# Decode attention over a 4096-long cache: the value blocks 1 to 30 are issued from ScalarE's DMA queue, the key blocks and the rest stay on SyncE's

## The chip, the cores and the metric

The kernel runs on one core of a Trainium2 chip. The metric is the device time of one execution in microseconds (us), median over several runs. Trace times below are microseconds from the start of the profiled execution's span. In the profile's rows PE is TensorE, PEld its weight loads, DVE is VectorE, ACT is ScalarE, POOL is GpSimd, and SP is SyncE, which here only issues DMAs. A row with a q behind the engine (SPq, ACTq) is the engine's instruction stream issuing a DMA, not the transfer itself.

## What is computed

One decode step of a transformer block: an adaptive layer norm, attention of 4 queries (one for each batch entry) with 32 heads of 128 over a cache of 4096 keys and values, an output projection, a second adaptive layer norm and a small SiLU feed-forward. All of it is float32.

```python
mod = (silu(c) @ w_mod).reshape(B, 6, 1, -1)        # B = 4
sa, ca, ga, sb, cb, gb = (mod[:, i] for i in range(6))
h = layernorm(x) * (1 + ca) + sa
q = (h @ wq).reshape(B, 1, H, Dh).transpose(0, 2, 1, 3)          # H = 32, Dh = 128
scores = einsum("bhqd,bhkd->bhqk", q, k_cache) * Dh ** -0.5      # 4096 keys
o = einsum("bhqk,bhkd->bhqd", softmax(scores), v_cache)
x = x + ga * (o.transpose(0, 2, 1, 3).reshape(B, 1, H * Dh) @ wo)
h = layernorm(x) * (1 + cb) + sb
x = x + gb * (silu(h @ w1) @ w2)
```

The caches are 268 MB each, and every byte of them is used once.

## The kernel before

The attention is cut into N = 32 blocks. Block n holds four heads (`t = n // 4`) of one batch entry (`b = n % 4`). Its keys `k{n}` and its values `v{n}` are each one load of 8 MiB: 128 partitions of 64 KB, where a partition holds 128 consecutive positions of one head. The function `load` issues such a load through `fetch` (L84).

**Slots.** All large data share one pool of three buffers of 64 KB a partition (tag `kv`, class `Slot`), handed out in turn. In order of time the slots go to `wm`, `wq`, `k0`, `v0`, `k1`, `v1`, `k2`, `v2` and so on, then `wo` and `w12`. So `v{n+1}` takes the slot of `k{n}`, and `k{n+2}` the slot of `v{n}`. A load is issued when the last reader of the slot's earlier content is done. That gives two moments in each block, named here R(n) and P(n):

- R(n): VectorE's last reduce of `k{n}` ends. Then `v{n+1}` can be issued.
- P(n): TensorE's last matmul on `v{n}` (`vsum`, L324) ends. Then `k{n+2}` can be issued.

**A block, step by step.** The key product is split by positions: VectorE multiplies positions 40 to 127 with the query (L271, the moment at which it starts is named S(n)) and reduces them (L276). GpSimd multiplies positions 0 to 39 (L271), and VectorE reduces these as well. At R(n) all scores are there. `rowmax`, `bmax` and `negmax` form the negative maximum, and `softexp` (L298) the exponentials on ScalarE, which GpSimd spreads into the zero-padded tiles `pz` (L302). TensorE multiplies 96 of the 128 value positions (`pv`, L339). For the first 32 positions GpSimd multiplies values by weights (L314) and adds them down in three steps (L318); `vsum` (L324) is TensorE's short end of it. After each second block `gather` (L350, L356) collects the output.

**Order.** The schedule is manual: every engine executes its instructions in the order in which the code emits them, and a waiting instruction holds up everything behind it on its engine. All loads of the caches and the weights are issued by SyncE. ScalarE issues four small loads of `c` at the start (L123), four small loads of `x` in block 28 (L404), and two of the four stores of the output. The loads of `wo` follow `v31`, and those of `w1` and `w2` come last.

Of the kernel before, what the change touches and what calls it, by code (L numbers as in the profile page):

```python
# [17 lines left out]
def kernel(  # L18
# [13 lines left out]
    nc = tc.nc  # L32
# [9 lines left out]
    NJ = HP * S // P  # L42
# [13 lines left out]
    N = B * NT  # L56
# [22 lines left out]
            names = " ".join(f"a{i}" for i in range(len(shape)))  # L79
            return v.rearrange(f"p ({names}) -> p {names}", **{f"a{i}": s for i, s in enumerate(shape)})  # L80

    def fetch(t, src, *cuts):
        for lo, hi in zip(cuts, cuts[1:]):
            nc.sync.dma_start(t[:, lo:hi], src[:, lo:hi])  # L84

    kt, vt = {}, {}

    def load(dst, cache, name, n, *cuts):
        t, b = divmod(n, B)
        dst[n] = Slot(f"{name}{n}").take(NJ, Dh)  # L90
        src = cache[b, HP * t : HP * (t + 1)].rearrange("h (p j) d -> (h p) j d", p=QW)
        fetch(dst[n], src, *(cuts or (0, NJ)))

    def load_k(n, *cuts):
        load(kt, kc, "k", n, *cuts)

    def load_v(n):
        load(vt, vc, "v", n)

    wmv = wm.rearrange("(p k) n -> p k n", p=P)  # L100
    wqv = wq.rearrange("(p k) n -> p k n", p=P)
# [26 lines left out]
    wqt = s1.take(NK, H * Dh)  # L128
    nc.sync.dma_start(wqt, wqv)
    load_k(0)  # L130

    ident = const.tile([P, P], F32, name="ident")
# [123 lines left out]
    def make_qb(n):  # L256
        if n % B == 0:
            m = work.tile([P, B, Dh], F32, tag="o", name=f"qm{n}", bufs=1)
            for b in range(B):
                nc.scalar.activation(m[:, b, :], qn, AF.Copy, scale=sel[:, n + b : n + b + 1])  # L260
            p = psum([P, B, Dh], "q", 2)
            nc.tensor.matmul(p, blk.rearrange("p i x -> p (i x)"), m, start=True, stop=True)
            for b in range(B):
                qb[n + b] = p[:, b, :]
        qw[n] = work.tile([P, Dh], F32, tag="qw", name=f"qw{n}")
        nc.scalar.activation(qw[n], qb[n], AF.Copy)  # L266
# [3 lines left out]
    def mult(eng, src, n, lo, hi):  # L270
        eng.tensor_mul(  # L271
            kt[n][:, lo:hi, :], kt[n][:, lo:hi, :], src[n].unsqueeze(1).to_broadcast([P, hi - lo, Dh])
        )

    def red(n, lo, hi):
        nc.vector.tensor_reduce(sc[n][:, lo:hi], kt[n][:, lo:hi, :], axis=AX.X, op=ALU.add)  # L276

    def rowmax(n):
        nm[n] = work.tile([P, 1], F32, tag="rm", name=f"rm{n}")
        nc.vector.tensor_reduce(nm[n], sc[n], axis=AX.X, op=ALU.max)  # L280

    def bmax(n):
        p = psum([P, P], "mx", 2)
        nc.tensor.transpose(p, nm[n].to_broadcast([P, P]), ident)  # L284
        nm[n] = p

    def negmax(n):
        m = work.tile([P, HP], F32, tag="hx", name=f"hx{n}")
        nc.vector.tensor_reduce(m, nm[n].rearrange("p (i x) -> p i x", i=HP), axis=AX.X, op=ALU.max)  # L289
        nc.vector.tensor_mul(m, m, hn)  # L290
        nm[n] = work.tile([P, 1], F32, tag="nm", name=f"nm{n}")
        nc.vector.tensor_reduce(nm[n], m, axis=AX.X, op=ALU.add)  # L292

    def softexp(n):
        t, b = divmod(n, B)
        if b == 0:
            rs[t] = work.tile([P, B], F32, tag="rs", name=f"rs{t}")
        nc.scalar.activation(sc[n], sc[n], AF.Exp, bias=nm[n], accum_out=rs[t][:, b : b + 1])  # L298
        for h in range(2):
            f = first(n) if h == 0 else 0  # L300
            m = HG - f
            nc.gpsimd.tensor_mul(  # L302
                pz[h][:, f * W : HG * W].rearrange("p (g x) -> p g x", g=m)[:, :, E:].rearrange("p g (i j) -> p g i j", i=HP),
                sc[n][:, JJ * (HG * h + f) : HG * JJ * (h + 1)].rearrange("p (g j) -> p g j", j=JJ)
                .unsqueeze(2).to_broadcast([P, m, HP, JJ]),
                hm.unsqueeze(1).unsqueeze(3).to_broadcast([P, m, HP, JJ]),
            )

    def first(n):
        return NV // JJ if n < N - 2 else 0  # L310

    def vmult(n):
        if first(n):
            nc.gpsimd.tensor_mul(  # L314
                vt[n][:, :NV, :], vt[n][:, :NV, :], sc[n][:, :NV].unsqueeze(2).to_broadcast([P, NV, Dh])
            )
            for m in (NV // 2, NV // 4, JJ):
                nc.gpsimd.tensor_add(vt[n][:, :m, :], vt[n][:, :m, :], vt[n][:, m : 2 * m, :])  # L318

    def vsum(n):  # L320
        t, b = divmod(n, B)
        q, a = divmod(b, 2)
        o = (1 - a) * E
        nc.tensor.matmul(  # L324
            po[t, q][0:W, :], hs[:, o : o + W], vt[n][:, :JJ, :].rearrange("p j d -> p (j d)"),
            start=False, stop=a == 1,
        )
# [20 lines left out]
    def gather(t, q):  # L348
        o = work.tile([P, JJ, Dh], F32, tag="o", name="o", bufs=1)
        nc.vector.tensor_mul(  # L350
            o, po[t, q].rearrange("p (j d) -> p j d", j=JJ), jm.unsqueeze(2).to_broadcast([P, JJ, Dh])
        )
        if q == 0:
            od[t] = psum([P, Dh], "od", 1)
        s = work.tile([P, Dh], F32, tag="lnu", name="s", bufs=1)
        nc.vector.tensor_reduce(s, o.rearrange("p j d -> p d j"), axis=AX.X, op=ALU.add)  # L356
        nc.tensor.matmul(od[t], spick[:, 2 - 2 * q : 2 - 2 * q + P], s, start=q == 0, stop=q == 1)  # L357
# [3 lines left out]
    def norm(t):  # L361
        p = psum([P, B], "mx", 2)
        nc.tensor.matmul(p, blk.rearrange("p i x -> p (i x)"), rs[t], start=True, stop=True)
        m = work.tile([P, B], F32, tag="dx", name="dx")
        nc.vector.tensor_mul(m, p, xm)
        rd[t] = work.tile([P, 2], F32, tag="rd", name="rd")
        nc.vector.tensor_reduce(rd[t][:, 0:1], m, axis=AX.X, op=ALU.add)
        nc.vector.reciprocal(rd[t][:, 1:2], rd[t][:, 0:1])

    def spread(t):  # L370
        on = work.tile([P, R, QW], F32, tag="lnu", name="on", bufs=1)
        nc.vector.tensor_scalar(
            on, od[t].rearrange("p (x r) -> p r x", r=R), rd[t][:, 1:2], None, op0=ALU.mult
        )
        ot = work.tile([P, R, W], F32, tag="ot", name="ot", bufs=1)
        nc.vector.transpose(ot, on)
        nc.vector.tensor_copy(oz[:, t], ot[:, :, :B])
# [11 lines left out]

    make_qb(0)  # L390
    load_v(0)
    for n in range(N):
        t, b = divmod(n, B)
        if n < N - 2:
            load_k(n + 1)
        elif n == N - 2:
            load_k(n + 1, 0, NJ // 2, NJ)
        else:
            so = Slot("wo")
            wot = so.take(NT, R, D)  # L400
            fetch(wot, wov, 0, NT // 2, NT - 2, NT - 1, NT)
        if n == N - B:
            for g in range(G):
                nc.scalar.dma_start(xg[W * g : W * g + B, :], xr[:, g * P : (g + 1) * P])  # L404
        sc[n] = work.tile([P, NJ], F32, tag="sc", name=f"sc{n}")
        if n + 1 < N:
            mult(nc.gpsimd, qw, n, 0, NA)
            mult(nc.vector, qb, n, NA, NJ)
            make_qb(n + 1)
            if n and first(n - 1):  # L410
                vsum(n - 1)
            red(n, NA, NJ)
        else:
            for lo in (0, NJ // 2):
                mid, hi = lo + NL // 2, lo + NJ // 2
                mult(nc.gpsimd, qw, n, lo, mid)
                mult(nc.vector, qb, n, mid, hi)
                red(n, mid, hi)
        if n and b == 0:
            gather(t - 1, 1)  # L420
        if b == 2:
            gather(t, 0)
        if n + 1 < N:
            red(n, 0, NA)
        else:
            for lo in (0, NJ // 2):
                red(n, lo, lo + NL // 2)
        if n and b == 0:
            spread(t - 1)
        rowmax(n)  # L430
        bmax(n)
        negmax(n)
        softexp(n)
        if n + 1 < N:
            load_v(n + 1)
        else:
            s2 = Slot("w12")
            w1t = s2.take(NK, F)
            w2t = s2.take(NI, D)
            fetch(w1t, w1v, 0, 2, 3, 4)  # L440
            fetch(w2t, w2v, 0, 4, 8, 11, 12, 13, 14)
        if b == B - 1:
            norm(t)
        vmult(n)
        pv(n)
# [74 lines left out]
```

## Time and profile before

| what | value |
| --- | --- |
| median of 3 runs | 1323.12 us (1322.9 to 1323.14) |
| profiled execution, its own time | 1323.02 us |
| its span, first to last instruction | 1321.1 us |
| busy: VectorE, GpSimd, TensorE, ScalarE | 1011.0, 844.9, 381.0, 45.2 us |
| moved by DMA | 567.66 MB, mean 430 GB/s |

The profiled execution takes 1.9 us more than its span; this is what lies around the first and the last instruction. The page cuts the span into 40 slices and says for each how busy the 16 DMA engines were and what they moved. The chain of work lists the pieces that ended last, followed back from the end. The timeline lists instructions in order of time, and in brackets the idle time ahead of one with what ended it.

### The profile page before, as it was taken

The page shows a single profiled execution, that of the slowest core. Times are in us where ns is not written, and L with a number is a line of the kernel's source. Part 1 is how long each engine was busy: PE and PEld are TensorE (multiplying, and loading weights), DVE is VectorE, ACT ScalarE, POOL GpSimd, SP SyncE. Part 2 cuts the span into 40 slices and gives each one's busy share as a digit, 9 for nine tenths or more (in the row PEclk, how much of TensorE's full clock was granted, in tenths as well). Part 3 has the DMA queues.
Part 4 walks back from the last instruction along what each step waited for, and adds up shares of the span by engine and source line. Part 5 has one row for each costly group of instructions (what it writes and reads, how often), then busy time and mean ns, then how long its engine had stood idle before and what let it go on. Part 6 is the DMA issues. An engine that isn't in the chain of part 4 may idle for free.

```text
span 1321.1 us, 5438 instructions
## 1 busy us (share of the span) xinstructions
PE 381.0 (29%) x2114; PEld 98.8 (7%) x2114; DVE 1011.0 (77%) x362; ACT 45.2 (3%) x148; POOL 844.9 (64%) x231
## 2 busy tenths in 40 slices
PE   3421133222222233222322322233321223322047
PEld 0100000000000000000000000000000000000013
DVE  2378877877888777898778788787779877787982
ACT  1100000000000000000000000000000000000001
POOL 1236787575678756577865756877565786657550
PEclk9855666665566666566666556666655666655569
DMA  9999999999999999999999999999999999999998
GB/s 413 443 415 442 439 421 437 437 427 437 433 431 435 435 431 433 433 435 433 433 427 437 435 429 435 439 429 429 439 429 433 441 429 429 434 437 429 425 425 341
DMA packets 12282, 567.66 MB, mean 430 GB/s; under 512 B 1441, under 2 KB 1505, under 8 KB 2273
## 3 DMA queue, kind: packets, MB, share of 16 engines
q1 hardware_dynamic: 12048, 567.29, 99.5%
q8 instruction: 17, 0.28, 0.1%
q14 instruction: 9, 0.07, 0.0%
q0 software_dynamic: 128, 0.01, 0.0%
q10 hardware_dynamic: 80, 0.02, 0.0%
HBM read 567.30 MB, written 0.01 MB: 429 GB/s over the span
## 4 chain that ended last, share of the span: by engine, by line
DVE 39%; DMA 32%; POOL 19%; another core or an unknown queue 4%; PE 3%; issue 2%; ACT 1%; DVEq 0%; POOLq 0%; ACTq 0%
DMA k<-in_A_k_cache_dram 29%; DVE sc L276 21%; DVE k L271 14%; POOL v L318 9%; POOL v L314 8%; DMA w<-in_B_w_dram 3%; PE po L324 2%; DVE s L356 1%; POOL pz L302 1%; POOL k L271 1%; DVE o L350 1%; ACT sc L298 1%; PE mx L284 1%; DVE hx L289 0%
## 5 line engine op out<-in xcount | busy, mean ns | idle before, releaser
L276 DVE TENSOR_REDUCE sc<-k 128x88 f32<-128x11264 f32 (+2 forms) x66 | 554.4, 8422 | 1.1
L271 DVE TENSOR_TENSOR k<-k,q 128x11264 f32<-128x11264 f32 (+1 forms) x33 | 378.4, 11467 | 217.9 <-DMA k<-in_A_k_cache_dram 217.9
L271 POOL TENSOR_TENSOR k<-k,qw 128x5120 f32<-128x5120 f32 (+1 forms) x33 | 356.2, 10796 | 53.1 <-DMA k<-in_A_k_cache_dram 53.1
L302 POOL TENSOR_TENSOR pz<-sc,hm 128x128 f32<-128x128 f32 (+1 forms) x64 | 31.5, 512 | 378.7 <-ACT sc L298 378.7
L339 PE MATMUL po<-v,pz 128*32 128x512 f32 x1568 | 239.5, 775 | 44.3 <-POOL pz L302 44.2
L318 POOL TENSOR_TENSOR v<-v 128x2048 f32<-128x2048 f32 (+2 forms) x90 | 244.6, 2717 | 7.1
L314 POOL TENSOR_TENSOR v<-v,sc 128x4096 f32<-128x4096 f32 x30 | 211.0, 7033 | 0.0
L324 PE MATMUL po<-v,hs 128*32 128x512 f32 x60 | 57.4, 1061 | 249.4 <-POOL v L318 249.4
L284 PE MATMUL mx<-ident,rm 128*128 128x128 f32 x32 | 14.5, 454 | 385.9 <-DVE rm L280 385.9
L357 PE MATMUL od<-s,spick 128*128 128x128 f32 x32 | 12.2, 484 | 217.5 <-DVE s L356 217.5
L339 PEld LDWEIGHTS po<-v,pz 128*32 128x32 f32 x1568 | 56.3, 138 | 205.7 <-issue 154.1
L284 PEld LDWEIGHTS mx<-ident,rm 128*128 128x128 f32 x32 | 5.8, 182 | 417.4 <-issue 272.3
L298 ACT ACTIVATE sc<-sc,nm 128x128 f32<-128x128 f32 x32 | 12.8, 401 | 694.8 <-DVE nm L292 694.8
L266 ACT ACTIVATE qw<-q 128x128 f32<-128x128 f32 x32 | 8.9, 277 | 505.1 <-DVE k L271 446.7
L324 PEld LDWEIGHTS po<-v,hs 128*32 128x32 f32 x60 | 5.4, 140 | 276.1 <-POOL v L318 276.1
L357 PEld LDWEIGHTS od<-s,spick 128*128 128x128 f32 x32 | 7.8, 303 | 244.2 <-DVE s L356 129.3
L289 DVE TENSOR_REDUCE hx<-mx 128x4 f32<-128x128 f32 x32 | 9.3, 292 | 19.7 <-PE mx L284 19.7
L350 DVE TENSOR_TENSOR o<-po,jm 128x512 f32<-128x512 f32 x16 | 10.9, 682 | 9.1 <-PE po L339 9.1
L356 DVE TENSOR_REDUCE s<-o 128x128 f32<-128x512 f32 x16 | 16.3, 1020 | 0.6
L190 PE MATMUL q<-wm 128*32 128x512 f32 x48 | 10.0, 723 | 20.5 <-DVE wm L178 20.5
L198 DVE TENSOR_TENSOR wm<-q,hm 64x256 f32<-64x256 f32 (+1 forms) x8 | 4.1, 549 | 9.2 <-PE q L190 8.3
L260 ACT ACTIVATE qm<-qn,sel 128x128 f32<-128x128 f32 x32 | 10.1, 387 | 0.0
(95 smaller groups left out, 137.6 us busy)
## 6 DMA issues: line engine op xcount, KB each, us to landing
k<-in_A_k_cache_dram SPq DMA_DIRECT2D x2, 4096.0 KB
wm<-in_w_mod_dram SPq DMA_DIRECT2D x1, 6144.0 KB
wo<-in_A_wo_dram SPq DMA_DIRECT2D x1, 4096.0 KB
wo<-in_A_wo_dram SPq DMA_DIRECT2D x1, 2048.0 KB
wo<-in_A_wo_dram SPq DMA_DIRECT2D x2, 1024.0 KB, 33.0
w<-in_B_w_dram SPq DMA_DIRECT2D x2, 1024.0 KB
w<-in_B_w_dram SPq DMA_DIRECT2D x1, 1792.0 KB
w<-in_B_w_dram SPq DMA_DIRECT2D x2, 896.0 KB
```

The lines of the kernel that those rows point to most:

```text
L271: eng.tensor_mul(kt[n][:, lo:hi, :], kt[n][:, lo:hi, :], src[n].unsqueeze(1).to_broadcast([P, hi - lo, Dh]))
L276: nc.vector.tensor_reduce(sc[n][:, lo:hi], kt[n][:, lo:hi, :], axis=AX.X, op=ALU.add)
L284: nc.tensor.transpose(p, nm[n].to_broadcast([P, P]), ident)
L298: nc.scalar.activation(sc[n], sc[n], AF.Exp, bias=nm[n], accum_out=rs[t][:, b : b + 1])
L302: nc.gpsimd.tensor_mul(pz[h][:, f * W : HG * W].rearrange("p (g x) -> p g x", g=m)[:, :, E:].rearrange("p g (i j) -> p g i j", i=HP), sc[n ...
L314: nc.gpsimd.tensor_mul(vt[n][:, :NV, :], vt[n][:, :NV, :], sc[n][:, :NV].unsqueeze(2).to_broadcast([P, NV, Dh]))
L318: nc.gpsimd.tensor_add(vt[n][:, :m, :], vt[n][:, :m, :], vt[n][:, m : 2 * m, :])
L324: nc.tensor.matmul(po[t, q][0:W, :], hs[:, o : o + W], vt[n][:, :JJ, :].rearrange("p j d -> p (j d)"), start=False, stop=a == 1,)
L339: nc.tensor.matmul(po[t, q][W * g : W * (g + 1), :], pz[h][:, o : o + W], vt[n][:, JJ * j : JJ * (j + 1), :].rearrange("p j d -> p (j d)") ...
L350: nc.vector.tensor_mul(o, po[t, q].rearrange("p (j d) -> p j d", j=JJ), jm.unsqueeze(2).to_broadcast([P, JJ, Dh]))
L356: nc.vector.tensor_reduce(s, o.rearrange("p j d -> p d j"), axis=AX.X, op=ALU.add)
L357: nc.tensor.matmul(od[t], spick[:, 2 - 2 * q : 2 - 2 * q + P], s, start=q == 0, stop=q == 1)
```

## The change

`fetch` and `load` get the issuing engine as an argument. `load_v` hands over ScalarE for blocks 1 to 30, and SyncE for `v0` and `v31`. The call of `load_v(n + 1)` moves ahead of `softexp(n)`, so that on ScalarE the issue stands in front of block n's exponential. Sizes, slots and the work of the other engines are the same.

```diff
-    def fetch(t, src, *cuts):
+    def fetch(t, src, *cuts, eng=nc.sync):
         for lo, hi in zip(cuts, cuts[1:]):
-            nc.sync.dma_start(t[:, lo:hi], src[:, lo:hi])
+            eng.dma_start(t[:, lo:hi], src[:, lo:hi])
...
-    def load(dst, cache, name, n, *cuts):
+    def load(eng, dst, cache, name, n, *cuts):
...
-        fetch(dst[n], src, *(cuts or (0, NJ)))
+        fetch(dst[n], src, *(cuts or (0, NJ)), eng=eng)
...
     def load_k(n, *cuts):
-        load(kt, kc, "k", n, *cuts)
+        load(nc.sync, kt, kc, "k", n, *cuts)
...
     def load_v(n):
-        load(vt, vc, "v", n)
+        load(nc.scalar if 0 < n < N - 1 else nc.sync, vt, vc, "v", n)
...
         negmax(n)
-        softexp(n)
         if n + 1 < N:
             load_v(n + 1)
-        else:
+        softexp(n)
+        if n + 1 == N:
             s2 = Slot("w12")
```

On SyncE's queue, in the first blocks, the rows of the values 1 and up go, and the keys follow one another. The names are those of the loads' destinations, with the block's number behind k or v.

```order
 L84 DMA v0_259<-in_A_v_cache_dram 128x16384
 L84 DMA k1_261<-in_A_k_cache_dram 128x16384
-L84 DMA v1_283<-in_A_v_cache_dram 128x16384
 L84 DMA k2_314<-in_A_k_cache_dram 128x16384
-L84 DMA v2_336<-in_A_v_cache_dram 128x16384
 L84 DMA k3_366<-in_A_k_cache_dram 128x16384
-L84 DMA v3_394<-in_A_v_cache_dram 128x16384
 L84 DMA k4_425<-in_A_k_cache_dram 128x16384
```

A value load no longer stands between two key loads; SyncE now waits for the slots of the keys alone.

On ScalarE, in the same blocks, `qw` is the copy of the query for GpSimd's product, and `sc`, `rs` and `nm` are the scores, their sums and the negative maxima of the exponential.

```order
 L266 ACTIVATE qw1_266<-q_255 128x128
+L84 DMA v1_279<-in_A_v_cache_dram 128x16384
 L298 ACT_TABLE_LOAD
-L298 ACTIVATE sc0_263,rs0_279<-sc0_263,nm0_277 128x128
+L298 ACTIVATE sc0_263,rs0_281<-sc0_263,nm0_277 128x128
 L266 ACTIVATE qw2_319<-q_255 128x128
-L298 ACTIVATE sc1_316,rs0_279<-sc1_316,nm1_331 128x128
+L84 DMA v2_333<-in_A_v_cache_dram 128x16384
+L298 ACTIVATE sc1_316,rs0_281<-sc1_316,nm1_331 128x128
 L266 ACTIVATE qw3_371<-q_255 128x128
```

The issue of the next block's values stands between the query's copy and the exponential of the block at hand.

## The prediction

> **What bounds the kernel now.** I read the page first (busy shares, DMA line, chain), then the stretches in the middle, then the chain in order of time, and last the rows of the DMA issues, with what the first multiply of each block waits for.
>
> ```profile
> q1 hardware_dynamic: 12048, 567.29, 99.5%
> q10 hardware_dynamic: 80, 0.02, 0.0%
> DVE 39%; DMA 32%; POOL 19%; another core or an unknown queue 4%; PE 3%; issue 2%; ACT 1%; DVEq 0%; POOLq 0%; ACTq 0%
> ...
> 564.00:642.00 78.00, 21.12 (x118) 4.82 (x110) 61.96 (x17) 2.72 (x11) 55.33 (x16) 0.61 1.00 434
> 642.00:719.00 77.00, 19.68 (x106) 5.00 (x106) 62.47 (x23) 1.53 (x6) 52.74 (x14) 0.58 1.00 432
> ```
>
> The last two rows are two stretches of two blocks each: the DMA share (the number ahead of the rate) is 1.00 and the rate 433 GB/s, while VectorE works 62 of 78 us. No DMA engine pauses. 433 GB/s over 16 engines is 27.1 GB/s each, so a row of 64 KB takes one engine 2.42 us, and a block's load (128 rows, 8 for each engine) 19.4 us. Two blocks carry four loads, 77.5 us.
>
> The chain shows a second limit of almost the same length. This is one turn of it, block 14 to block 16:
>
> ```profile
> 600.29 11.90 DVE k L271
> 612.21 11.89 DVE sc L276
> 624.10 0.61 DVE o L350
> ...
> 625.75 5.40 DVE sc L276
> 633.44 0.97 POOL pz L302 x2
> 634.41 7.00 POOL v L314
> 641.48 4.54 POOL v L318
> ...
> 649.84 1.93 PE po L324 x2
> 651.79 26.16 DMA k<-in_A_k_cache_dram
> 678.07 11.90 DVE k L271
> ```
>
> ```profile
> 611.34 0.33 SPq L84 DMA_DIRECT2D k<-in_A_k_cache_dram  x1
> 631.17 0.33 SPq L84 DMA_DIRECT2D v<-in_A_v_cache_dram  x1
> 651.79 0.33 SPq L84 DMA_DIRECT2D k<-in_A_k_cache_dram  x1
> 668.58 0.33 SPq L84 DMA_DIRECT2D v<-in_A_v_cache_dram  x1
> 689.20 0.33 SPq L84 DMA_DIRECT2D k<-in_A_k_cache_dram  x1
> 639.35 11.89 DVE L271 TENSOR_TENSOR k<-k,q 128x11264 f32<-128x11264 f32 x1 [6.58 <-DMA k<-in_A_k_cache_dram]
> 649.75 10.98 POOL L271 TENSOR_TENSOR k<-k,qw 128x5120 f32<-128x5120 f32 x1
> ```
>
> The issues give the moments directly: S(14) = 600.29, R(14) = 631.17 (`v15` is issued), P(14) = 651.79 (`k16` is issued), S(16) = 678.07. So the turn is 30.88 (key product and reduces) + 20.62 (exponential, GpSimd's value work, the last matmul) + 26.28 (`k16`, from issue to use) = 77.78 us. Odd blocks take less: 639.35 to 668.58 is 29.23, with 20.62 to 689.20 behind it, 49.85 against 51.50. The turn is as long as four loads because the key load waits in the single queue until the values ahead of it are through: 26.28 holds 19.4 of its own transfer. The reader should see that slots, not SyncE, decide when loads are issued, and that the key load has no slack: whatever makes `k16` land later makes the turn longer.
>
> **Does a second queue share the engines row by row?** The start has both queues in use.
>
> ```profile
> 0.75 0.40 SPq L126 DMA_DIRECT2D wm<-in_w_mod_dram  x1
> 1.04 1.87 ACTq L123 DMA_DIRECT2D wm<-in_c_dram  x4
> ACT L174 <- DMA wm<-in_c_dram: 18.1, 1, 18.1
> POOL k L271 <- DMA k<-in_A_k_cache_dram: 53.1, 1, 53.1
> 58.24 11.03 POOL k L271
> ```
>
> ScalarE's four loads of `c` hold 8 KB together, were issued by 2.91 us and landed only at 18.1. Its queue counts 80 packets for ten such loads (four of `c`, four of `x`, two stores) of 4 rows each, 40 rows: each row has a second, small packet behind it, which I take for the signal of its completion. An engine that carries one row of each load of `c` therefore serves 8 packets. Beside them runs `wm`, whose rows of 48 KB take 1.82 us. Eight turns, one row of SyncE's for each small packet, are 14.5 us, and 2.91 + 14.5 is 17.4, against 18.1 seen. So the engines alternate, one packet of a queue for one of the other, and the completion needs a turn too.
>
> A rule of the Trainium skill speaks against row by row: DMA: Bandwidth & Descriptors, section Queues, rings and completion order, lets an engine go round the queues by packets of typically 9 to 17 descriptors, and drain one before it switches. A load here gives an engine 8 rows and a completion, 9 in all, so by that rule a key load that has begun would finish undisturbed and the sum below would be zero. The trace does not agree: eight small packets would then have gone in one turn or two, not in 15 us.
>
> **The change, part by part.**
>
> *Removed from SyncE*: 30 issues of 0.33 us. SyncE waits for slots between them, and R(n) lies 20.6 us ahead of P(n), so no key load ever waited behind a value issue that was not ready. Worth nothing.
>
> *Added on ScalarE*: 30 issues ahead of the exponential.
>
> ```profile
> L404 ACTq DMA_DIRECT2D xg<-in_A_x_dram x4: 255/306/306, 1136.5 to 1137.5; - x4
> 632.62 0.16 DVE L292 TENSOR_REDUCE nm<-hx 128x1 f32<-128x4 f32 x1
> ```
>
> About 0.3 us each. It can go at 631.17, when the slot is free, and the exponential waits for the maximum until 632.78: 1.6 us of cover, so zero. Without that cover it would be 0.3 us for each of 14 turns, 4 us. Behind a waiting issue stands only the exponential of the same block, which needs the same reduce.
>
> *Moved: the value transfers.* Bytes and slots are equal; what changes is who gets the engines when both kinds are pending. In one queue `k16` had the engines to itself once it began. Now `v16`, issued at R(15), takes every second turn. The price is the number of value rows that slip in between the rows of `k16`.
>
> How much of `k16` is left when `v16` is issued? Today `v16` follows `k16` by 16.8 us (651.79 to 668.58), which is 6.9 rows: one row and the completion remain, two value rows slip in, 4.8 us. But R(15) can come earlier: VectorE idles 6.58 us ahead of block 15 for its keys, and the odd blocks, with the shorter turn, gain on the even ones. The floor is GpSimd: its key product starts at 649.75, ends 10.98 later, and the 5.40 us reduce puts R(15) at 666.1, 14.3 us after `k16`. That is 5.9 rows; two rows and the completion remain, three value rows, 7.3 us.
>
> What does a key load need by itself, from issue to use? At the start, `wm`, `wq` and `k0` (6.29 + 8.39 + 8.39 MB, 53.3 us at 433 GB/s) are issued from 0.75 and used at 58.24: 4.2 us beyond the transfer. The other bound is the end:
>
> ```profile
> 1318.18 0.67 SPq L494 DMA_DIRECT2D out_dram<-w  x2
> ```
>
> The last 2 KB store is issued by 1318.85, and the span ends at 1321.1: 2.3 us at most. So a key load alone takes 21.7 to 23.6 us, and with values slipping in 26.5 (21.7 + 4.8) to 30.9 (23.6 + 7.3). I take the middle, 28.7, since nothing in the rows is nearer to one end. Then a turn is 51.5 + 28.7 = 80.2 us.
>
> ```profile
> 135.82 11.90 DVE k L271
> ...
> 1221.39 11.89 DVE L271 TENSOR_TENSOR k<-k,q 128x11264 f32<-128x11264 f32 x1 [7.99 <-DMA k<-in_A_k_cache_dram]
> ```
>
> From block 2 to block 30 there are 14 turns in 1085.57 us, 77.54 each. At 80.2 they cost 14 x 2.66 = 37 us more.
>
> ```profile
> 87.41 0.33 SPq L84 DMA_DIRECT2D v<-in_A_v_cache_dram  x1
> 96.90 11.89 DVE L271 TENSOR_TENSOR k<-k,q 128x11264 f32<-128x11264 f32 x1 [7.88 <-DMA k<-in_A_k_cache_dram]
> ```
>
> *Start.* `v1`, issued at R(0), now shares with `k1`, which is used 9.5 us later: some three rows and the completion are left, four value rows, 9.7 us. Block 1 then starts at 106.6 instead of 96.90 and ends 29.23 later; with about 1.5 us for the maximum, VectorE is free for block 2 at 137.3 instead of 135.82, so 1.5 us remain of it.
>
> *End.* The last part is limited by DMA: `v31`, `wo`, `w1` and `w2` follow `k31` in SyncE's queue. `k31` belongs to the odd blocks, which by then have gained: it lands about 32 us after `k30` instead of 38.7 (half of 77.54), which gives back 7 us: VectorE's block of 30.88 with the maximum is all that then lies between them.
>
> Sum: 1.5 + 37 - 7 = 31.5 us on the span of 1321.1, so 1352.6; with 1.9 around it 1354.5, from a profiled execution of 1323.02, which lies at the median of 1323.12. I say 1354. Over its ends the same sum goes from 1.5 + 14 x 0.46 - 7, which is no loss, to 1.5 + 14 x 4.86 - 7 = 62.5 (1386).
>
> *Cover.* `v15` is issued at 631.17 and needed by GpSimd's L314 in block 15, about 40 us later. By itself it takes 21.7 to 23.6, and six shared rows still fit. If that cover goes, each missing microsecond lengthens the turn.
>
> **The rivals.**
>
> 1. *No change (within 3 us, 1323).* A turn also cannot be shorter than four loads, 77.5; if key loads land in 26 us or less on average, only the order of the bytes changes. It needs at most one value row slipped in (21.7 + 2.4 = 24.1 to 23.6 + 2.4 = 26.0), that is, R(15) 17 us or more after P(14) throughout. For it: odd keys today have 19.8 us (611.34 to 631.17). Against it: even keys have 16.8 and no slack. Engines that stay with one load would give the same time.
> The Trainium skill has this result as a rule: the same page, section Issuing engines are not separate DMA queues, says that transfers of all queues interleave on the same 16 engines and that only the issuing time is saved.
> 2. *A little slower (1326 to 1340).* Two value rows and the short 21.7: 26.5 us, a turn of 78.0; or engines that idle a microsecond or so in each turn between the end of one load and the next issue.
> 3. *Much slower (over 1376).* The upper end, 30.9, or further rows slipped in at the head of the key load while the earlier values are unfinished.
> 4. *Faster (1319).* 567.66 MB at 433 GB/s are 1311 us; the span has 10 more, most of them the first and last microseconds. A second queue could fill only dips such as this one ahead of the last loads:
>
> ```profile
> 1272.00:1276.00 4.00, 0.00 (x0) 0.00 (x0) 4.00 (x2) 0.00 (x0) 0.00 (x0) 0.50 0.77 332
> 1276.00:1280.00 4.00, 0.00 (x0) 0.00 (x0) 4.00 (x2) 0.00 (x0) 0.00 (x0) 0.50 0.92 387
> ```
>
> They miss 1.2 us. With the rest that could be filled I put it at 4 us at best, and it decides only if the key loads land no later than now.
>
> **How the numbers follow.** The forecast (1340 to 1376) has 0.65, no change 0.11, a little slower 0.13, much slower 0.06, faster 0.05. The range 1326 to 1376 holds the forecast and the second rival, 0.78; I widen it to 1325 for the slow edge of no change. A difference of 0.2% (2.6 us) is about the least that a measurement of this kernel can tell. Faster by more: 0.05; within: 0.11; slower: 0.84.
>
> **What the profile after would show.** In the middle stretches the DMA share falls to about 0.97 (77.5 of 80.2) with the rate near 420 GB/s. Even key loads take 28 to 29 us from issue to use, and odd ones less. Block starts alternate, near 48 us from odd to even and 32 from even to odd, instead of 38.7 evenly. VectorE's idle time for keys is gathered ahead of the even blocks. If the share stays at 1.00 and starts stay even, the slipped rows cost nothing and the first rival is right. If the share falls but key loads take 26 us, the engines idle for another reason. I would be wrong most of all if the engines do not alternate between two large loads as they do between a large and a small one.

## The result, and the profile after

The changed kernel takes 1359.36 us (median of 6 runs, 1355.34 to 1369.1) against 1323.11 before (6 runs, 1322.9 to 1323.22). The ratio is 1.0281, with a 95% interval from 1.0247 to 1.0314: slower by 36 us. The forecast was 1354 in a range from 1325 to 1376. The runs of the changed kernel also spread over 13.8 us, against 0.3 before.

The profiled execution after took 1361.25 us, with a span of 1359.3. These lines of its page stand against those of before: the values now fill a second queue (q10), and the shares of the chain are much the same.

```profile
span 1359.3 us, 5437 instructions
q1 hardware_dynamic: 7728, 315.63, 54.5%
q10 hardware_dynamic: 4400, 251.68, 43.4%
DVE 37%; DMA 28%; POOL 22%; PE 5%; issue 4%; another core or an unknown queue 3%; ACT 1%; ACTq 0%; DVEq 0%; POOLq 0%
```

Two turns of two blocks in the changed kernel, as stretches; the last two columns are the DMA share and GB/s. Before, they read 1.00 and 432 to 434.

```profile
592.30:672.30 80.00, 21.46 (x106) 5.02 (x106) 61.08 (x17) 2.71 (x10) 54.10 (x15) 0.59 0.98 419
672.30:752.50 80.20, 20.94 (x106) 5.23 (x106) 63.22 (x23) 1.54 (x6) 54.04 (x15) 0.59 0.99 419
```

And the first of them in the timeline of the changed kernel, from the issue of `k14` to that of `k16`, with the starts of blocks 14 to 16 sorted in:

```profile
592.26 0.33 SPq L84 DMA_DIRECT2D k<-in_A_k_cache_dram  x1
606.74 0.33 ACTq L84 DMA_DIRECT2D v<-in_A_v_cache_dram  x1
620.77 11.89 DVE L271 TENSOR_TENSOR k<-k,q 128x11264 f32<-128x11264 f32 x1 [12.50 <-DMA k<-in_A_k_cache_dram]
627.26 0.33 SPq L84 DMA_DIRECT2D k<-in_A_k_cache_dram  x1
651.66 0.34 ACTq L84 DMA_DIRECT2D v<-in_A_v_cache_dram  x1
654.70 11.89 DVE L271 TENSOR_TENSOR k<-k,q 128x11264 f32<-128x11264 f32 x1 [1.44 <-DMA k<-in_A_k_cache_dram]
672.27 0.33 SPq L84 DMA_DIRECT2D k<-in_A_k_cache_dram  x1
700.35 11.89 DVE L271 TENSOR_TENSOR k<-k,q 128x11264 f32<-128x11264 f32 x1 [10.18 <-DMA k<-in_A_k_cache_dram]
```

Read the brackets first. Before, VectorE waited 5.5 to 8.2 us for the keys of every block from 1 to 30. Now it waits 12.50, then 1.44, then 10.18: blocks come in pairs, 33.9 us from 620.77 to 654.70 and 45.7 to 700.35. `k14` is issued at 592.26, and `v14`, the values of the same block, 14.5 us behind it; `k14` is used at 620.77. From block 8 on, every even block has the same 14.5 us. At first it is the odd blocks 1 and 3 that are late (46.0 us from block 2 to block 3); this turns over between blocks 4 and 6. `k14` takes 28.5 us from issue to use, `k15` 27.4. In the mean from block 6 on the even keys take 28.5 and the odd ones 27.1, against 25.7 and 27.7 before: the even keys have become 2.8 us slower, about what a turn has grown by.

Where do 3 us a turn go? Not to slower engines throughout. Three neighbouring stretches of the changed kernel:

```profile
588.00:600.00 12.00, 1.92 (x2) 0.18 (x2) 9.74 (x1) 0.00 (x0) 11.92 (x3) 0.50 0.96 393
600.00:648.00 48.00, 10.75 (x53) 2.65 (x53) 33.54 (x10) 0.77 (x3) 28.26 (x8) 0.57 1.01 435
648.00:660.00 12.00, 6.07 (x37) 1.65 (x41) 9.83 (x6) 1.66 (x6) 6.08 (x3) 0.57 0.88 355
```

For 48 us, with one or with both queues at work, the rate is 435 GB/s, as before. It drops around 592, where an even key load is issued, and around 652, where an odd block's values are. At both moments the last rows of the loads pending were ending when the next was issued. The single packets of the trace (one row on one engine each) show it: the last rows of `v13` end between 592.2 and 593.9, `k14` is issued at 592.26, and its first row starts 0.95 us after that. The engines ran dry for a short time, twice in a turn.

The packets also add up to the loss. From block 6 to block 30 a turn is 2.7 us longer than before. The engines stand idle for 1.5 us of it, and 1.1 us is taken by some 33 rows a turn that last about 3.0 us instead of 2.42, two for each engine: mostly the first one behind each dry moment.

### The profile page after: what moved, and what is told of

It reads as the page before. It is cut to its first block, busy times and chain, and to the rows that moved or that the text cites. A ratio compares the mean times of both kernels' runs of the same rounds, so it can differ in the third digit from the quotient of the medians.

```text
span 1359.3 us, 5437 instructions
## 1 busy us (share of the span) xinstructions
PE 384.3 (28%) x2114; PEld 100.2 (7%) x2114; DVE 1012.0 (74%) x362; ACT 45.2 (3%) x148; POOL 844.7 (62%) x231
## 4 chain that ended last, share of the span: by engine, by line
DVE 37%; DMA 28%; POOL 22%; PE 5%; issue 4%; another core or an unknown queue 3%; ACT 1%; ACTq 0%; DVEq 0%; POOLq 0%
DMA k<-in_A_k_cache_dram 27%; DVE sc L276 20%; DVE k L271 13%; POOL v L318 9%; POOL v L314 8%; POOL k L271 3%; PE po L324 2%; POOL pz L302 1%; DMA wm<-in_c_dram 1%; DVE s L356 1%; PE q L190 1%; PE po L339 1%; ACT sc L298 1%; DVE o L350 1%
## 5 line engine op out<-in xcount | busy, mean ns | idle before, releaser
L276 DVE TENSOR_REDUCE sc<-k 128x88 f32<-128x11264 f32 (+2 forms) x66 | 555.5, 8424 | 40.9 <-POOL k L271 39.8
L339 PE MATMUL po<-v,pz 128*32 128x512 f32 x1568 | 244.4, 789 | 44.3 <-POOL pz L302 44.2
L284 PE MATMUL mx<-ident,rm 128*128 128x128 f32 x32 | 14.5, 453 | 380.5 <-DVE rm L280 380.5
```

What stands on the lines that cost most here:

```text
L339: nc.tensor.matmul(po[t, q][W * g : W * (g + 1), :], pz[h][:, o : o + W], vt[n][:, JJ * j : JJ * (j + 1), :].rearrange("p j d -> p (j d)") ...
```

## Experiments

**What was to be told apart.** My theory: value rows go ahead of key rows that are needed sooner, so key loads land late and in pairs with the values, and the order of the bytes costs the time. The first rival: the place of the issue ahead of the exponential. The second: two queues with large loads lower the rate by themselves, whatever their order.

**1. The place alone.** All loads on SyncE again, the call left ahead of the exponential.

```diff
-        load(nc.scalar if 0 < n < N - 1 else nc.sync, vt, vc, "v", n)
+        load(nc.sync, vt, vc, "v", n)
```

> Only the place of the value issue in the code is changed (ahead of the exponential); all loads stay on SyncE. Theory (value rows slip in between key rows, and the two-block turn has no slack): no second queue, no slipping, 1323 us within 1. Rival 'place' (the earlier issue holds up the exponential): up to 1359. Rival 'second queue lowers the rate': 1323.

1323.18 us, ratio 1.000 (0.999 to 1.001). The earlier place in the code costs nothing while SyncE issues. Whether the issue holds up the exponential on ScalarE this run can't show, but the trace of the changed kernel can: from the issue of `v15` at R(14) to that of `k16` at P(14) are 20.61 us (651.66 to 672.27), the same as before (20.62, from 631.17 to 651.79). In no block up to 29 is it longer than before, so nothing is held up.

**2. Half of the values, odd or even.** The odd ones as shown, the even ones with `== 0`.

```diff
-        load(nc.scalar if 0 < n < N - 1 else nc.sync, vt, vc, "v", n)
+        load(nc.scalar if 0 < n < N - 1 and n % 2 == 1 else nc.sync, vt, vc, "v", n)
```

> Only the odd values (1, 3 .. 29) go to ScalarE's queue. Theory: the odd key load is issued 19.8 us ahead of the odd value load in the kernel before, so all its rows are under way; at most the last row and the completion are met, and the odd blocks have 1.65 us of slack in each turn: 1322 to 1335 us, most likely 1326. Rival 'second queue lowers the rate': half of the loss, about 1341. Rival 'place': half, about 1341.

> Only the even values (2, 4 .. 30) go to ScalarE's queue. Theory: these are the ones that meet the even key loads of the long turn, two rows slipped in, so nearly the whole loss stays: 1345 to 1362 us. Rival 'second queue lowers the rate': half of the loss, about 1341, the same as with the odd ones. Rival 'place': the same half.

Even alone: 1365.2 us, 1.0308 (1.0283 to 1.0332), 3 us above the range expected. Odd alone: 1356.19 us, 1.0252 (1.0231 to 1.0272). Either half costs all of it, so the loss does not go by the number of loads, and the second rival's half is out. But my own expectation for the odd half failed. The timeline of the kernel with the odd values on ScalarE:

```profile
616.77 11.89 DVE L271 TENSOR_TENSOR k<-k,q 128x11264 f32<-128x11264 f32 x1 [3.11 <-DMA k<-in_A_k_cache_dram]
632.69 0.33 SPq L84 DMA_DIRECT2D k<-in_A_k_cache_dram  x1
647.66 0.33 ACTq L84 DMA_DIRECT2D v<-in_A_v_cache_dram  x1
661.47 11.89 DVE L271 TENSOR_TENSOR k<-k,q 128x11264 f32<-128x11264 f32 x1 [12.21 <-DMA k<-in_A_k_cache_dram]
695.34 11.89 DVE L271 TENSOR_TENSOR k<-k,q 128x11264 f32<-128x11264 f32 x1 [1.22 <-DMA k<-in_A_k_cache_dram]
```

Now the odd block is the late one: it starts at 661.47, 44.7 us after the even one, and the next 33.9 after it. I had taken the 19.8 us between odd keys and odd values as given by the odd blocks' shorter work. They are not: with the pairs formed the other way round, 15.0 us (632.69 to 647.66) are left. Which block of a pair is late is not fixed: it is the odd one here, and in the changed kernel the odd one up to block 3 and the even one from block 6 on.

**3. Two queues, split by block.** Keys and values of the odd blocks 3 to 29 on ScalarE's queue, everything else on SyncE's.

```diff
-        load(nc.sync, kt, kc, "k", n, *cuts)
+        load(nc.scalar if n % 2 == 1 and 1 < n < N - 1 else nc.sync, kt, kc, "k", n, *cuts)
-        load(nc.scalar if 0 < n < N - 1 else nc.sync, vt, vc, "v", n)
+        load(nc.scalar if n % 2 == 1 and 1 < n < N - 1 else nc.sync, vt, vc, "v", n)
```

> Keys and values of the odd blocks 3 to 29 go to ScalarE's queue, keys and values of all other blocks stay on SyncE's: as many bytes in the second queue as with the values alone, and both queues have loads pending at once. But a value load now stands behind the key load of its own block in the same queue, so it cannot take turns from its end; a key load shares only with the rest of the values of the block ahead, whose rows would have gone first in one queue as well. Theory (what costs is that values issued later slip in ahead of a key load's last rows, which makes key loads and values land in pairs): no loss, 1321 to 1330 us, block starts evenly 38.7 us apart. Rival 'two large loads pending in two queues cost by themselves' (rate, or engines out of step): 1350 to 1365 us as with the other splits.

1323.24 us, ratio 1.000 (0.999 to 1.001). The stretches and the block starts of this kernel:

```profile
564.00:642.00 78.00, 21.45 (x109) 4.96 (x106) 61.88 (x17) 2.71 (x10) 55.32 (x16) 0.58 1.00 433
642.00:719.00 77.00, 21.36 (x96) 5.30 (x100) 62.48 (x23) 1.54 (x6) 52.67 (x14) 0.58 1.00 434
```

```profile
639.59 11.89 DVE L271 TENSOR_TENSOR k<-k,q 128x11264 f32<-128x11264 f32 x1 [6.67 <-DMA k<-in_A_k_cache_dram]
678.30 11.89 DVE L271 TENSOR_TENSOR k<-k,q 128x11264 f32<-128x11264 f32 x1 [6.06 <-DMA k<-in_A_k_cache_dram]
716.99 11.89 DVE L271 TENSOR_TENSOR k<-k,q 128x11264 f32<-128x11264 f32 x1 [5.52 <-DMA k<-in_A_k_cache_dram]
```

Fourteen blocks, 28 of the 64 loads, are in the second queue and loads of both queues are pending at once, yet the share is 1.00, the rate 433 GB/s, and the starts are 38.7 us apart. Here a value load stands behind the keys of its own block, so it cannot go ahead of their end. This run decides against the second rival.

**4. Out of order in one queue.** The reverse test: everything on SyncE, but a part of the values is placed ahead of the last eighth of the keys. With `VA` one eighth or three eighths:

```diff
+    KA, VA = 7 * NJ // 8, 3 * NJ // 8
+    def load_mixed(n):
+        load(vt, vc, "v", n, 0, VA)
+        fetch(kt[n], source(kc, n), KA, NJ)
+        fetch(vt[n], source(vc, n), VA, NJ)
...
-            load_k(n + 1)
+            load_k(n + 1, 0, KA)
...
-            load_v(n + 1)
+            (load_mixed if n + 1 < N - 1 else load_v)(n + 1)
```

> All loads on SyncE, one queue. Keys 1 to 30 first get seven eighths; the last eighth is issued at R(n), behind the first eighth of the next values, and the rest of the values behind it. So as many bytes as one 64 KB row an engine (2.42 us) of the values go ahead of the key load's end, in a fixed order. Theory (bytes taken out of order use up the lead: today the key load has about 6 us of transfer left when R(n) comes, 8.2 us to its use): 2.4 us of keys and 2.4 us of values still fit into 6 us, so no loss but the two extra cuts of a block, priced by the 7 us that three extra cuts of the values cost in one queue: 1324 to 1338 us. Rival 'only two queues at once do harm': the same.

> The same with three eighths of the values (7.3 us) ahead of the last eighth of the keys, still one queue on SyncE. Theory: 2.4 + 7.3 us no longer fit into the 6 us that are left at R(n), so the engines run dry for some 3 us and start again, 3 to 5 us in each of 30 blocks: 1400 to 1475 us. Rival 'only two queues at once do harm': as with one eighth, 1324 to 1338 us.

One eighth: 1346.35 us, 1.0181 (1.0156 to 1.0206), 8 us above the range. Three eighths: 1447.35 us, 1.0936 (1.0918 to 1.0954), within it. A stretch of two blocks with one eighth ahead, and then one with three eighths:

```profile
573.10:652.50 79.40, 20.32 (x120) 4.62 (x111) 61.74 (x16) 2.72 (x10) 55.31 (x15) 0.59 1.00 426
```

```profile
580.00:668.00 88.00, 21.41 (x106) 4.84 (x106) 64.43 (x20) 1.54 (x6) 57.42 (x17) 0.58 0.93 396
```

With one eighth the share is still 1.00 and the rate is lower, 426 GB/s. Rows that take longer can do that: the 8 KB rows last 0.32 us in the mean, where an eighth of 2.42 is 0.30. I had priced the cuts too low; the packets hold a little idle time too, some 0.4 us a turn. With three eighths the share falls to 0.93, and idle engines are 6.6 of the 8.2 us by which a turn is longer than before (blocks 6 to 30): the engines run dry in one queue. Both runs make the same number of loads and move the same bytes; they differ in the values that go ahead, and with them in the sizes of the value rows (8 and 56 KB, or 24 and 40). The 101 us between the two are the price of 4.84 us of values more ahead of the keys, in 30 blocks.

**5. Smaller rows.** If the engines take turns row by row, the size of a row is the share that a queue gets. Values in four loads of 16 KB rows, then the keys instead, and the small value rows in one queue as a control. The cuts of the values are the same, for blocks 1 to 30.

```diff
-            load_k(n + 1)
+            load_k(n + 1, 0, NJ // 4, NJ // 2, 3 * NJ // 4, NJ)
```

> Values 1 to 30 on ScalarE, each in four loads whose rows are 16 KB instead of 64 KB. Theory: an engine gives the values 0.6 us a turn instead of 2.42, and a completion almost nothing, so what slips into the end of a key load falls from 4.8 to 7.3 us to 1.2 to 1.8: key loads take 25 to 26 us, the turn is again limited by its four loads, 1321 to 1330 us. Rival 'second queue lowers the rate': more switches, 1359 or more.

> Keys 1 to 30 on SyncE in four loads with rows of 16 KB; values on ScalarE with rows of 64 KB. Theory: each small key row or completion left when the value load begins now waits for a whole value row; with a quarter of the key load left (8 small rows and 1 or 2 completions) all 8 value rows go first, up to 19 us instead of 5, and the turn grows by 5 to 14 us: 1400 to 1530 us. Rival 'second queue lowers the rate': as the changed kernel, 1355 to 1370.

> Control for the two runs with rows of 16 KB: the kernel before, all on SyncE, with values 1 to 30 in four loads of 16 KB rows. If small rows and their completions cost nothing by themselves: 1322 to 1327 us, so that the 1369 us with two queues come from the sharing. If they do: about 45 us more, 1365 us.

Small key rows: 1516.82 us, 1.1465 (1.1418 to 1.1511), as expected; the control with small value rows in one queue: 1330.48 us, 1.0055 (1.004 to 1.007), 3 us above the range for rows that cost nothing. Small key rows in one queue were not run. In the kernel with small key rows one odd load looks like this in the timeline: from its first issue to its use are 39.2 us.

```profile
882.53 1.65 SPq L84 DMA_DIRECT2D k<-in_A_k_cache_dram  x3
921.78 11.89 DVE L271 TENSOR_TENSOR k<-k,q 128x11264 f32<-128x11264 f32 x1 [23.16 <-DMA k<-in_A_k_cache_dram]
```

Small value rows with two queues: 1368.68 us, 1.0339 (1.0322 to 1.0356), where I had expected 1321 to 1330. The turns worked: in this kernel a load of keys is issued at 677.34 and used at 701.87, 24.5 us. But the time went elsewhere. From the chain of this kernel, in order of time:

```profile
651.03 5.17 ACTq L84
...
656.24 1.60 ACTq L84
...
658.42 0.50 ACT sc L298 x2
```

ScalarE issues four loads here, and the second issue lasts 5.17 us and the third 1.60. The maximum is ready at 652.3, but the exponential comes at 658.42, so 6 us are added behind R(n). From `v5` to `v29` the four issues of an odd block's values take 4.0 to 8.2 us together, those of an even block's mostly 1.7. The turn (block 2 to block 30, 1132.1 us over 14) is 80.9 us, no shorter than with large rows. The cover that the prediction names (a 0.3 us issue within 1.6 us) does not hold for several issues.

**6. A shorter way from R(n) to P(n).** All 128 value positions on TensorE, nothing of the values on GpSimd, with two queues and, as a control, with one.

```diff
     def first(n):
-        return NV // JJ if n < N - 2 else 0
+        return 0
```

> The changed kernel, with all 128 value positions on TensorE (GpSimd's products and sums of the first 32 and their short end are gone, the result is the same sum). Theory: P(n) comes some 8 us earlier, the turn is about 30.9 + 12.5 + 28.5 = 72 us, below the 77.5 us of its four loads; value rows still slip in but no longer set the time: 1320 to 1328 us. Rival 'second queue lowers the rate': 1355 to 1362 as before.

> The kernel before (one queue) with the same edit: all 128 value positions on TensorE. Control for the run with two queues. Both theories: DMA was the limit and stays it, 1321 to 1325 us.

One queue: 1324.18 us, 1.0009 (1.0 to 1.0018). Two queues: 1372.34 us, 1.0376 (1.0341 to 1.041). My expectation failed by 44 us, and this was the experiment on the slack that the prediction's sum rests on. Timeline and stretches of the kernel with two queues:

```profile
823.17 0.33 SPq L84 DMA_DIRECT2D k<-in_A_k_cache_dram  x1
841.46 0.33 ACTq L84 DMA_DIRECT2D v<-in_A_v_cache_dram  x1
853.92 0.33 SPq L84 DMA_DIRECT2D k<-in_A_k_cache_dram  x1
862.98 11.89 DVE L271 TENSOR_TENSOR k<-k,q 128x11264 f32<-128x11264 f32 x1 [18.10 <-DMA k<-in_A_k_cache_dram]
893.86 0.33 ACTq L84 DMA_DIRECT2D v<-in_A_v_cache_dram  x1
```

```profile
830.00:884.00 54.00, 10.49 (x67) 2.94 (x67) 33.79 (x11) 0.77 (x3) 12.21 (x3) 0.56 0.99 426
890.00:895.00 5.00, 0.02 (x1) 0.05 (x1) 4.76 (x5) 0.00 (x0) 0.00 (x0) 0.50 0.41 131
```

The keys issued at 823.17 share at first with the values still under way, later with those of 841.46, and are used only at 862.98, after 39.8 us. VectorE then works on them until 893.86. In this time the other two slots are filled, and no slot is free: up to 884 the rate is 426 GB/s, and from 890 to 895 it is 131. A shorter turn does not help, because the keys, issued earlier, share for longer. What is used up is the lead. In one queue the next load is always issued some microseconds before the one ahead ends (`v15` 8.2 us before `k15` is used). Values fetched ahead of the keys delay the block, and at the end of that block everything that fits into the slots has already landed.

**7. Issue behind the exponential**, with two queues.

```diff
-        if n + 1 < N:
-            load_v(n + 1)
         softexp(n)
-        if n + 1 == N:
+        if n + 1 < N:
+            load_v(n + 1)
+        else:
```

> Values 1 to 30 on ScalarE, but issued behind the exponential, some 2.3 us later. Theory: the value load meets the key load about one row (2.42 us) later, so one value row fewer slips in; even key loads take about 26 instead of 28.4 us and the turn 78 to 79 us instead of 80.5: 1325 to 1345 us. Rival 'second queue lowers the rate': no difference to the changed kernel, 1355 to 1365. Rival 'place': 14 turns with 0.3 us less, 1355.

1511.08 us, 1.1427 (1.1404 to 1.1451): none of the expected numbers, and no test of them. The waits of SyncE's queue in this kernel, longest first (us in total, times, longest):

```profile
SPq L84 <- PE po L324: 769.4, 24, 47.4
SPq L84 <- DVE rm L280: 228.7, 8, 32.7
```

In the changed kernel the second of these rows reads 34.2 us, 2 times. The edit made more key issues wait for VectorE's last reduce, which comes 14.5 us later than the matmul on the values; these loads were evidently handed another slot. There are six, every fourth from `k8` to `k28`, and in each case the values of the same block are issued just 1.8 us behind the keys, against 14.5 us or more in the changed kernel: the two loads seem to have changed slots. So this run tells that the place of a call can decide which slot a load gets, and leaves open what 2 us of delay alone would do.

## Why the prediction was right, and where not

**The turn.** Block 2 starts at 135.21 and block 30 at 1261.84 (rows below), 80.47 us a turn; the prediction had 80.2. The 14 turns cost 41.1 us more than before, against 37. Its two parts hold as well: the values are issued 14.5 us behind the even keys, the floor that GpSimd sets (14.3 forecast), and the key load takes 28.5 us (28.7). The signs named for the profile came: share 0.98, 419 GB/s, and starts 46 and 34 us apart in turn (48 and 32 forecast).

That the middle of the range came out for the key load is in part luck. It stood for two or three value rows slipped in and 21.7 to 23.6 us for the load alone. The packets show exactly two rows (4.84 us) in 11 of the 13 even key loads from `k6` to `k30`, and more only in `k10` and `k28`. So a load alone takes about 23.7 us (28.5 less 4.84), the upper of the two bounds. In it are slower first rows behind the dry moment, which the sum did not name.

**Start and end.** From the timeline of the changed kernel, and the chain of the kernel before:

```profile
135.21 11.89 DVE L271 TENSOR_TENSOR k<-k,q 128x11264 f32<-128x11264 f32 x1 [0.69 <-DMA k<-in_A_k_cache_dram]
...
1261.84 11.89 DVE L271 TENSOR_TENSOR k<-k,q 128x11264 f32<-128x11264 f32 x1 [12.43 <-DMA k<-in_A_k_cache_dram]
...
1294.27 4.96 DVE L271 TENSOR_TENSOR k<-k,q 128x4608 f32<-128x4608 f32 x1
```

```profile
1253.82 4.96 DVE k L271
```

The start costs -0.6 us instead of +1.5. The end gives back 2.2 us (99.7 from block 30 to the end of the span before, 97.5 after) instead of 7. This is the step that was mis-sized: I let block 31 follow 38.7 us behind block 30, but before, it follows after 32.4 already (1221.39 to 1253.82), and after it is 32.4 too. `k31` is loaded in two halves, and VectorE, which starts with the first half, has no idle time in front of it in either trace: its own work sets the 32.4. The row was in the trace. The sum by the two profiles is -0.61 + 41.06 - 2.25 = 38.2 us, from a span of 1321.1 to one of 1359.3.

**The reason.** The engines alternate between two large loads as they do between a large and a small one: in the packets of the changed kernel each engine carries a row of `k14`, a row of `v14`, a row of `k14` and a row of `v14` in turn between 608.3 and 618.5, at 2.42 us each. Small key rows cost 194 us, and small value rows bring keys down to 24.5. The Trainium skill's rule on draining 9 to 17 descriptors at a time (DMA: Bandwidth & Descriptors, Queues, rings and completion order) is not borne out here. The Trainium skill's other rule, that transfers of all queues interleave and only issuing time is saved (Issuing engines are not separate DMA queues), names the fact behind the loss, but not its price: by block it is 0, by kind 36 us.

What fell is the account of slack. By the prediction the turn's 51.5 us plus the key load set the time; from that I had expected, before the runs, that a shorter turn cures the loss and that odd blocks have slack. With 8 us less in the turn the time rose to 1372, and odd values alone cost 33 us. The sum holds as a description of the chain, but the key load's 28.5 us is no constant to be added: with 8 us less in the turn it was 39.8 in the block shown, and the engines still ran dry. The number was right for a narrower reason than the true one, the loss of the order in which loads are needed. That is shown by the split by block, which keeps the order with two queues and costs nothing, and by the runs in one queue, where more values ahead of the keys bring the dry moments back.

**Left open.** What sets which block of a pair is late, why pairs form at all, and why single issues last several microseconds was not tried. No version beat the kernel before; the split by block equals it.

## What to carry to other kernels

In this kernel DMA is saturated, and the one queue works as a priority list: loads land in the order in which they are needed. A second queue gave that order away, row for row, and the rate did not rise (435 GB/s at best, 432 to 434 before). Before loads are split over queues, ask for each which later-needed rows may now pass earlier-needed ones, and how much lead is left when the next issue comes. If two queues are wanted, split so that what is needed first stays ahead in its own queue.

## What the runs showed of the hardware

- The share that a queue gets goes by the size of its rows: 8 MiB of keys took 24.5 us (`k16`), 28.5 (`k14`) or 39.2 (`k19`) from issue to use, with values in 16 KB rows, both in 64 KB rows, or keys in 16 KB rows. The even blocks from 6 on lie between 23.1 and 25.6, between 27.4 and 31.3, and between 31.9 and 40.3.
- The issue of a DMA is not always 0.3 us. The second of four issues in a row on ScalarE lasted 5.17 us, and all that stood behind it waited.
- A dry moment costs more than its idle time. `k14`, issued as the engines ran dry, had its first row start 0.95 us after the issue, and the first row of each engine took about 3.0 us against 2.42 for the rows behind it. The 12 us around the two dips of a turn have 393 and 355 GB/s, against 435 between them.
